# Block-sparse attention with a maxout layer: a written-out task order, and 86 tasks on other engines

## The chip, the core and the metric

The kernel runs on one core of a Trainium2 chip. The core has TensorE (PE in the profile; its weight loads are listed apart as PEld), VectorE (DVE), ScalarE (ACT), GpSimd (POOL) and SyncE (SP), which here only issues DMAs. Each engine works through its own list of instructions in order; between engines there are only semaphore waits. The metric is the device time in microseconds of one execution. "Span" is the time from the first to the last instruction in the profile of one execution; the execution's own time is a little longer.

## The reference

Attention over 4 batches, 8 heads, 768 positions and head dimension 64. Each query sees the keys within 15 positions of it, and, for all 24 blocks of 32 positions, one key that is the maximum over the block and one value that is the mean over the block, with log(32) added to the block's score. Behind it stands a maxout layer on 3072 tokens.

```python
k_sum = k.reshape(B, H, nb, block, D).max(axis=3)          # block = 32, nb = 24
v_sum = v.reshape(B, H, nb, block, D).mean(axis=3)
scores_l = scale * q @ k.T, kept where |pos_q - pos_k| < 16
scores_s = scale * q @ k_sum.T + log(block)
a = softmax(concat([scores_l, scores_s]))
x = (a @ concat([v, v_sum])) with heads side by side         # 3072 x 512
h1, h2 = x @ w1, x @ w2                                      # 512 x 1024 each
out = maximum(h1, h2) @ w_out                                # 1024 x 512
```

## The kernel before

The program is written as 776 tasks. A task has an engine, an estimated duration, a function that issues its instructions, a label, and the buffers that it reads and writes (`Plan.op`, line 123). Buffers come out of rings of slots (`Ring`, line 42): six for loaded k and q (`kqf`), four for loaded v (`vf`) and for weights (`wf`), four for turned k (`kx`) and q (`qx`), eight PSUM banks (`banks`), and so on. `Plan.run` (line 155) walks over time in steps of 0.02 us, starts on every idle engine the task of the best priority whose inputs and slots are free by its estimates, gives its buffers their slots, and so gets an order. It then calls the tasks' functions in that order (line 187). An engine's instruction list is the order in which the functions were called; waits between engines follow from the data and from the slots.

Labels carry batch and head pair (b, hp: "k12" is k of batch 1, head pair 2), and for later work batch and a third of the positions (grp, 256 positions each). The stages are:

- **Loads** on SP, in one queue: `load k`, `load q` (lines 362, 367), `load v` (373) for each batch and head pair, 384 KB each; `load w0`, `load w1` (693), twice each, 1 MB (columns 0 to 511 of w1 and of w2, then columns 512 to 1023 of both); `load wo0`, `load wo1` (726). A load needs a free slot, that is, the cast of what stood there before must be done.
- **Preparing k and q** (`prep`, 515): `cast` to bf16, `turn` (transposes on TensorE, 543, or for some pairs of batches 2 and 3 by DMA, 505 and 510), `place` (PSUM to `kx` or `qx`), `max k` (block maxima, VectorE, 562), `wrap`, `tails` and `sums k` (copies inside `kx`).
- **Preparing v** (`cast_v`, 384; `spread_v`, 392): `cast v`, for batches 1 to 3 `ones` (a memset on GpSimd, 402), `odd v` (three shifted copies), `sums` (block means on TensorE, 427 and 432, and a copy out) and `all sums` (the means laid beside every window). The sums of batches 1 to 3 need all four casts of v of their batch.
- **Attention**: `scores` (TensorE, 600, for batch 0 with the mask added by 591), `exp` (ScalarE, 625), `mask` (VectorE, 632, batches 1 to 3), `values` (TensorE, 648), `inv` and `x` (VectorE, 659 and 661: the division by the sum), `turn x` (TensorE, 674, or DMA, 666) and `xt` (copy of the turned x out of PSUM).
- **Weights**: `wd n` = w2 - w1 for a quarter n of the columns (700), `w1b n` (cast), `turn w1 n` (714; for n = 2 on f32, straight from the loaded `wf`), `w1t n` (copy out of PSUM), `wo n` (cast of w_out), and `w1o` = w1 @ w_out (741, two TensorE tasks and one copy for each quarter). The layer is computed as relu(x @ wd) @ w_out + x @ w1o.
- **The layer** (`maxout`, 749): `hidden b grp n` (757), `relu` (ScalarE, 762), `out` (`out_part`, 772: one TensorE task on w1o, line 778, and two on w_out, line 785), `copy out` and the store (806, 808). The last tile of all is cut into column groups of 256, 128 and 128.
- **Fillers**: 40 `idle` matmuls on zeros (829), put where TensorE has nothing else to do; all lie in the first 25 us.

Copies are made by one helper (`copy`, line 485), so that in the profile most casts, places and moves on all three engines carry line 490 and are told apart by their tiles.

`CFG` holds one letter for each group of copies, which chooses its engine, and priorities and corrections to them (`bump`), from which the planner makes the order.

Of the kernel before, what the change touches and what calls it, by code (L numbers as in the profile page):

```python
# [16 lines left out]
ACT = mybir.ActivationFunctionType  # L17
# [2 lines left out]

CFG = dict(
    smc="CCC",
    kd="....D..DD.DD", xd="D...DD.DD.DDDDDDDD", tus=(1.6, 1.0, 1.2), kc="ADDA", qc="APPP", kp="DADD", qp="DDDA",
    tl="AADA", od="DADP", se="DADA", sr="DPdP", vc="ADPA", sc=4, s0=4, ph=1, ph0=2, av=4, lkp="DDDA", lxt="DADAAD",
    idle=40, pz=1, wd="PPDD", w1b="DPFD", w1t="AAAA", wo="PAAD", xt="DDDDDA", kv=(0.2, 1.2, 4.2, 4.2), sp=0.7,
# [11 lines left out]
    },  # L37
)
ENG = {"D": "DVE", "A": "ACT", "P": "POOL"}


class Ring:
# [70 lines left out]
class Plan:  # L113
# [9 lines left out]
    def op(self, engine, us, fn, read=(), write=(), change=(), touch=(), behind=(), prio=0.0, label="", port=False):  # L123
        t = Task()
        t.engine, t.us, t.fn, t.label = engine, us, fn, label
        t.port = engine == "POOL" or port and engine == "DVE"
        t.prio = (prio + CFG["bump"].get(label, 0), len(self.tasks))
        t.new, t.behind = [*write, *change], behind
        t.deps = {w for b in (*read, *change) for w in b.writers}
        for b in t.new:  # L130
            b.writers.append(t)
        for b in (*read, *touch, *t.new):
            b.users.append(t)
        self.tasks.append(t)
        return t
# [19 lines left out]
    def run(self):  # L155
        waiting = {e: [] for e in self.LAG}
        for t in sorted(self.tasks, key=lambda t: t.prio):
            waiting[t.engine].append(t)
        busy = dict(self.BEGIN)
        self.held = {"POOL": 0.0, "DVE": 0.0}  # L160
        sent = [0.0] * self.DEPTH
        gate = Gate(1.0)
        order, tick = [], 0
        while len(order) < len(self.tasks):
            now = tick * 0.02
            for e, queue in waiting.items():
                if busy[e] > now or (e == "SP" and sent[-self.DEPTH] > now):
                    continue
                t = next((t for t in queue if self.ready(t, now)), None)
                if t is None:  # L170
                    continue
                t.start = now
                if e == "SP":
                    busy[e] = now + self.ISSUE
                    end = max(sent[-1], now + self.FIRST) + t.us
                    sent.append(end)
                    t.done = end + max(0.0, min(1.5, 0.6 * (end - 2.3), 0.4 * (14.0 - end)))
                else:
                    end = gate.end(now, t.us) if e == "PE" else now + t.us
                    busy[e] = t.done = end  # L180
                    if t.port:
                        self.held[e] = t.done
                queue.remove(t)
                order.append(t)
            tick += 1
            assert now < 1000, [t.label for q in waiting.values() for t in q]
        for t in order:
            t.fn()
        return order

# [2 lines left out]
def kernel(  # L193
# [14 lines left out]
    nc = tc.nc  # L208
    B, H, S, D = 4, 8, 768, 64
# [10 lines left out]
    op = plan.op  # L220
# [132 lines left out]
    kqin, kx, qx, xt = {}, {}, {}, {}  # L353
# [131 lines left out]
    def copy(engine, us, aps, label, port=True, halves=False, **kw):  # L485
        engine = ENG[engine]
        us = us if isinstance(us, float) else us[engine[0]]
        def fn():
            for o, i in [aps(0), aps(1)] if halves else [aps()]:
                {"DVE": nc.vector.tensor_copy, "ACT": nc.scalar.copy,  # L490
                 "POOL": nc.gpsimd.tensor_copy}[engine](out=o, in_=i)
        op(engine, us, fn, label=label, port=port, **kw)

    def on(e):
        return {"DVE": nc.vector, "POOL": nc.gpsimd}[e]
# [192 lines left out]
    def load_w12(half, prios, prio, prio_t):  # L688
        fs = []
        for w, at in zip((moe_w1, moe_w2), prios):  # L690
            f = Buf(wfr)
            fs.append(f)
            op("SP", 2.9, lambda f=f, w=w: nc.sync.dma_start(  # L693
                out=f.ap[:],
                in_=w.rearrange("(c p) n -> p c n", p=128)[:, :, 512 * half:512 * half + 512]),
               write=[f], prio=at, label=f"load w{half}")
        for n in (2 * half, 2 * half + 1):
            part = lambda f, at=256 * (n % 2): f.ap[:, :, at:at + 256]
            e = CFG["wd"][n]
            op(ENG[e], {"D": 1.23, "P": 2.3}[e], lambda n=n, part=part, e=e: on(ENG[e]).tensor_tensor(  # L700
                out=wd[n].ap[:], in0=part(fs[1]), in1=part(fs[0]), op=ALU.subtract),
               read=fs, write=[wd[n]], prio=prio + n % 2, port=True, label=f"wd {n}")
            whole = CFG["w1b"][n] == "F"
            if not whole:
                copy(CFG["w1b"][n], {"P": 1.05, "A": 1.06, "D": 0.75}, lambda n=n, part=part: (w1b[n].ap[:], part(fs[0])),
                     read=fs[:1], write=[w1b[n]], prio=prio + n % 2, label=f"w1b {n}")
            ps = Buf(banks, "x", 2 if whole else 1)

            def turn(n=n, ps=ps, whole=whole, part=part):
                src, to, one = (part(fs[0]), bank(ps, 1024), ident32) if whole else (  # L710
                    w1b[n].ap, bank(ps, 1024, BF16), identity)
                for f in range(2):
                    for c in range(KC):
                        nc.tensor.transpose(  # L714
                            out=to[:, (f * KC + c) * 128:(f * KC + c) * 128 + 128],
                            in_=src[:, c, 128 * f:128 * f + 128], identity=one[:])
# [184 lines left out]
```

## Time and profile before

| what | value |
|---|---|
| median of 3 runs | 170.58 us (170.07, 170.58, 171.06) |
| the profiled execution's own time | 170.39 us |
| span of the profiled execution | 168.7 us |
| granted TensorE clock | 1.00 |
| instructions in the profile | 4452 |
| HBM read, written | 25.17 MB, 6.29 MB |
| VectorE, ScalarE, GpSimd busy | 104.0, 93.0, 42.9 us |

The page of the profile gives busy times and shares of the span, the chain of work that ended last (each step followed back to what released it), groups of instructions by line with their mean duration, and DMA issues. In the chain, "SPq" is the time that SP's queue needs to issue a DMA, "DMA" the time until the data is there, "issue" the engine's own time between instructions. Matmul ends are modelled: two matmuls one behind the other overlap in the listing, so spacing from start to start says more than the listed length. The trace also has the moments at which each transfer landed; the first loads landed at 3.95 us (k00) to 18.90 (v03), the four weight loads at 22.61, 25.32, 28.29 and 30.93, then q10 31.99, k10 33.17, v10 34.55, k11 35.56, q11 36.54, wo0 39.22, wo1 42.04, v11 43.75, k12 44.76, q12 46.61, v12 48.33, q13 49.41, k13 50.53, v13 52.31, k20 54.06, q20 55.86, v20 56.96, k21 58.72, q21 59.80, v21 62.13, q22 63.18, k22 64.16, v22 66.61.

Medians of some durations on each engine, from the trace (us):

| task | VectorE | ScalarE | GpSimd |
|---|---|---|---|
| cast k | 0.59 | 1.05 | 0.94 |
| cast q, cast v | 0.55 | 0.83 | 0.83 |
| place k | 0.55 | 0.80 | |
| place q | 0.95 | 0.80 | |
| xt | 0.42 | 0.59 | |
| wrap, tails | 0.16, 0.25 | 0.21, 0.51 | 0.38, 0.51 |
| odd v 0, 1, 2 (batch 0) | 0.36, 0.66, 0.44 | 0.83, 0.72, 0.29 | 1.03, 0.71, 0.29 |
| all sums (batches 1 and 2) | 1.26 | | |
| wd, w1b | 1.22, 0.67 | | 2.36, 1.04 |
| wo | 0.69 | 1.05 | 1.04 |
| w1o (copy) | 0.69 | | |

### The profile page before, as it was taken

The page shows a single profiled execution, that of the slowest core. Times are in us where ns is not written, and L with a number is a line of the kernel's source. Part 1 is how long each engine was busy: PE and PEld are TensorE (multiplying, and loading weights), DVE is VectorE, ACT ScalarE, POOL GpSimd, SP SyncE. Part 2 cuts the span into 40 slices and gives each one's busy share as a digit, 9 for nine tenths or more (in the row PEclk, how much of TensorE's full clock was granted, in tenths as well). Part 3 has the DMA queues.
Part 4 walks back from the last instruction along what each step waited for, and adds up shares of the span by engine and source line. Part 5 has one row for each costly group of instructions (what it writes and reads, how often), then busy time and mean ns, then how long its engine had stood idle before and what let it go on. Part 6 is the DMA issues. An engine that isn't in the chain of part 4 may idle for free.

```text
span 168.7 us, 4452 instructions
## 1 busy us (share of the span) xinstructions
PE 158.6 (94%) x1819; PEld 104.4 (62%) x1819; DVE 104.0 (62%) x224; ACT 93.0 (55%) x146; POOL 42.9 (25%) x73
## 2 busy tenths in 40 slices
PE   4797896999999999999999999999999999999992
PEld 2665565998464655577484675865747658746661
DVE  6799997999569996758994744839438360000001
ACT  3767872789851766346185584681764716424420
POOL 7824889142215150036202010116020000000000
PEclk9999999999999999999999999999999999999999
DMA  5999999999999999999699999965753527011113
GB/s 170 314 316 283 336 389 376 304 348 342 301 294 216 264 334 292 189 239 162 128 271 334 260 203 194 241 155 116 200 102 99 125 59 163 0 62 73 55 62 124
DMA packets 69397, 35.82 MB, mean 212 GB/s; under 512 B 56577, under 2 KB 63361, under 8 KB 69377
## 3 DMA queue, kind: packets, MB, share of 16 engines
q1 hardware_dynamic: 65856, 29.38, 75.5%
q10 hardware_dynamic: 3520, 6.16, 11.6%
q8 instruction: 14, 0.23, 0.6%
q14 instruction: 7, 0.05, 0.1%
HBM read 25.17 MB, written 6.29 MB: 186 GB/s over the span
## 4 chain that ended last, share of the span: by engine, by line
PE 73%; SPq 9%; DVE 7%; DMA 7%; issue 2%; DVEq 0%
PE banks L757 24%; PE banks L785 22%; PE banks L778 10%; DMA wf<-in_moe_w_dram 7%; SPq L367 4%; PE banks L741 4%; PE banks L648 3%; PE banks L600 3%; SPq L373 3%; DVE vx L490 3%; PE banks L543 2%; SPq L693 2%; PE banks L714 1%; PE banks L674 1%; DVE qx L490 1%
## 5 line engine op out<-in xcount | busy, mean ns | idle before, releaser
L785 PE MATMUL banks<-wo,g 128*128 128x512 bf16 (+2 forms) x208 | 46.9, 363 | 0.0
L757 PE MATMUL banks<-xt,wd 128*128 128x256 bf16 x384 | 46.4, 273 | 0.0
L757 PEld LDWEIGHTS <-wd 128*128 128x128 bf16 x384 | 36.7, 98 | 6.5 <-issue 0.2
L762 ACT ACTIVATE g<-banks 128x512 bf16<-128x512 f32 x48 | 28.0, 602 | 14.2 <-PE banks L757 14.0
L794 ACT COPY o<-banks 128x512 f32<-128x512 f32 x23 | 13.5, 586 | 32.0 <-PE banks L785 31.0
L785 PEld LDWEIGHTS <-g 128*128 128x128 bf16 x208 | 18.4, 98 | 17.7 <-issue 0.2
L778 PE MATMUL banks<-w1o,xt 128*128 128x512 bf16 (+2 forms) x104 | 23.7, 363 | 0.0
L490 POOL CAST kqb<-kqf 128x768 bf16<-128x768 f32 x12 | 11.3, 942 | 37.5 <-PE banks L543 18.5
L625 ACT ACTIVATE pba<-banks 128x1024 bf16<-128x1024 f32 x16 | 16.4, 1025 | 6.0 <-PE banks L600 5.6
L632 DVE TENSOR_TENSOR pba<-pba,mask 128x1024 bf16<-128x1024 bf16 x12 | 8.5, 706 | 15.4 <-ACT pba L625 15.3
L490 DVE COPY o<-banks 128x128 f32<-128x128 f32 x2 | 0.6, 292 | 26.8 <-PE banks L785 26.8
L661 DVE TENSOR_TENSOR xs<-banks,inv 128x512 bf16<-128x512 f32 x24 | 16.3, 687 | 0.6
L778 PEld LDWEIGHTS <-xt 128*128 128x128 bf16 x104 | 9.8, 98 | 8.8
L562 DVE TENSOR_REDUCE ks<-kx 128x24 bf16<-128x768 bf16 x16 | 15.0, 945 | 0.1
L490 POOL CAST vx<-vf 128x768 bf16<-128x768 f32 x7 | 5.9, 843 | 22.5 <-DMA vf<-in_v_dram 22.4
L600 PEld LDWEIGHTS <-kx 64*128 64x128 bf16 x416 | 7.3, 96 | 6.7 <-issue 5.7
L490 ACT CAST kqb<-kqf 128x768 bf16<-128x768 f32 x9 | 7.9, 881 | 5.7 <-DMA kqf<-in_k_dram 2.0
L490 POOL COPY kx<-kx 128x32 bf16<-128x32 bf16 (+1 forms) x12 | 6.2, 520 | 16.3 <-DMA kx<-kqb 10.3
L829 PE MATMUL banks<-zeros 128*128 128x256 bf16 x40 | 8.4, 336 | 1.8 <-DVE zeros L826 1.8
L625 ACT ACTIVATE pbb<-banks 128x512 bf16<-128x512 f32 x16 | 9.6, 603 | 0.8 <-ACT o L794 0.8
L490 DVE COPY vx<-vx 64x3168 bf16<-64x3168 bf16 (+5 forms) x15 | 9.9, 676 | 0.2
L600 PE MATMUL banks<-qx,kx 64*128 64x64 bf16 (+2 forms) x416 | 9.4, 190 | 0.0
(85 smaller groups left out, 184.1 us busy)
## 6 DMA issues: line engine op xcount, KB each, us to landing
kqf<-in_k_dram SPq DMA_DIRECT2D x16, 384.0 KB, 6.7
kqf<-in_q_dram SPq DMA_DIRECT2D x16, 384.0 KB, 5.8
vf<-in_v_dram SPq DMA_DIRECT2D x16, 384.0 KB, 6.8
out_dram<-o ACTq DMA_DIRECT2D x19, 256.0 KB, 3.9
wf<-in_moe_w_dram SPq DMA_DIRECT2D x4, 1024.0 KB, 10.2
wf<-in_moe_w_out_dram SPq DMA_DIRECT2D x2, 1024.0 KB, 7.5
out_dram<-o ACTq DMA_DIRECT2D x4, 224.0 KB, 3.3
vx<-sums SPq DMA_DIRECT2D x4, 99.0 KB, 3.7
```

The costliest lines, as they stand in the source:

```text
L490: {"DVE": nc.vector.tensor_copy, "ACT": nc.scalar.copy, "POOL": nc.gpsimd.tensor_copy}[engine](out=o, in_=i)
L562: op("DVE", 0.95, lambda: nc.vector.tensor_reduce(out=ks.ap[:], in_=free(kt(), 128, [256, NM], [192, 2], [32, 2], [1, 32]), axis=AX.X, op= ...
L600: nc.tensor.matmul(out=bank(ps[i], 1024)[:, 512 * a + at + n0:512 * a + at + n1], lhsT=kx[b, hp].ap[r, 128 * t + 128:128 * t + 256], rhs=q ...
L625: op("ACT", (1.03, 0.6)[i], lambda: nc.scalar.activation(out=pv(), in_=bank(ps, 1024).rearrange("p (a c) -> p a c", a=2)[:, :, 0:64 * n], ...
L632: op("DVE", (0.69, 0.43)[i], lambda: nc.vector.tensor_tensor(out=pv(), in0=pv(), in1=m, op=ALU.mult), read=[mask_in], change=[pb], prio=pr ...
L661: op("DVE", 0.69, lambda: nc.vector.tensor_tensor(out=x.ap[:], in0=av()[:, :, :, 0:D], in1=inv.ap[:].to_broadcast([128, 2, 4, D]), op=ALU. ...
L757: nc.tensor.matmul(out=bank(ps)[:, 256 * s:256 * s + 256], lhsT=wd[n].ap[:, c, 128 * s:128 * s + 128], rhs=x.ap[:, c, :], start=(c == 0), ...
L762: op("ACT", 0.6, lambda n=n, ps=ps: nc.scalar.activation(out=g.ap[:, 2 * n:2 * n + 2, :].rearrange("p f n -> p (f n)"), in_=bank(ps), func ...
L778: nc.tensor.matmul(out=bank(ps, c1 - c0), lhsT=x.ap[:, c, sl], rhs=w1o[c].ap[:, cols], start=(c == 0), stop=False)
L785: nc.tensor.matmul(out=bank(ps, c1 - c0), lhsT=g.ap[:, f, sl], rhs=wo[f // 2].ap[:, f % 2, cols], start=False, stop=(f == FC - 1))
L794: nc.scalar.copy(out=aps()[0], in_=aps()[1])
L829: nc.tensor.matmul(out=bank(ps, 256), lhsT=zeros[:, 0:128], rhs=zeros[:], start=True, stop=True)
```

## The change

The planner still runs and still gives every buffer its slot. Then its order is thrown away: a tuple `ORDER` of the 776 task numbers says in which order the functions are called. A dictionary `done_by` names 86 tasks whose copy (for wd 1 and wd 3 the subtraction) is made by another engine than the letters in `CFG` say: 26 go from VectorE to ScalarE, 16 from VectorE to GpSimd, 13 from ScalarE to VectorE, 12 from GpSimd to VectorE, 12 from GpSimd to ScalarE, 7 from ScalarE to GpSimd. No instruction is added or removed.

```diff
 CFG = dict(
     smc="CCC",
+    done_by={
+        "cast v00": "DVE", "odd v000": "POOL", "odd v001": "ACT", "odd v002": "POOL", "odd v020": "DVE",
+        "odd v021": "DVE", "odd v022": "POOL", "odd v040": "ACT", "odd v041": "POOL", "odd v042": "ACT",
+        "cast v03": "DVE", "odd v060": "DVE", "wd 1": "DVE", "wd 3": "POOL", "w1b 3": "POOL", "w1t 3": "DVE",
+        "wo 2": "POOL", "cast k00": "DVE", "place k00": "ACT", "wrap k00": "POOL", "tails k00": "DVE",
+        "place q00": "ACT", "cast k01": "ACT", "cast q01": "ACT", "place k01": "DVE", "place q01": "ACT",
+        "cast k02": "POOL", "cast q02": "ACT", "place k02": "ACT", "wrap k02": "POOL", "place q02": "ACT",
+        "cast k03": "POOL", "cast q03": "DVE", "place k03": "ACT", "tails k03": "POOL", "xt 000": "ACT",
+        "xt 020": "ACT", "xt 001": "ACT", "xt 021": "ACT", "xt 002": "ACT", "cast v10": "DVE", "cast v11": "POOL",
+        "place k10": "ACT", "cast k11": "POOL", "place q11": "DVE", "xt 102": "ACT", "wrap k12": "ACT",
+        "tails k12": "DVE", "place q12": "ACT", "cast k13": "ACT", "place k13": "DVE", "wrap k13": "DVE",
+        "tails k13": "DVE", "place q13": "ACT", "cast v20": "ACT", "cast v22": "POOL", "cast v23": "DVE",
...
+        "cast q33": "ACT", "wrap k33": "ACT", "w1o 1": "ACT", "w1o 2": "ACT",
+    },
...
+ORDER = (
+    60, 12, 61, 6, 62, 14, 8, 15, 16, 2, 71, 4, 0, 3, 19, 72, 9, 13, 21, 23, 73, 128, 82, 129, 130, 17, 26, 25, 132,
...
+    763, 764, 765,
+)
...
             tick += 1
             assert now < 1000, [t.label for q in waiting.values() for t in q]
+        order = [self.tasks[i] for i in ORDER]
+        assert len(set(ORDER)) == len(self.tasks)
         for t in order:
+            t.engine = CFG["done_by"].get(t.label, t.engine) if t.engine in ENG.values() else t.engine
             t.fn()
         return order
...
             for o, i in [aps(0), aps(1)] if halves else [aps()]:
                 {"DVE": nc.vector.tensor_copy, "ACT": nc.scalar.copy,
-                 "POOL": nc.gpsimd.tensor_copy}[engine](out=o, in_=i)
+                 "POOL": nc.gpsimd.tensor_copy}[CFG["done_by"].get(label, engine)](out=o, in_=i)
...
-            op(ENG[e], {"D": 1.23, "P": 2.3}[e], lambda n=n, part=part, e=e: on(ENG[e]).tensor_tensor(
+            op(ENG[e], {"D": 1.23, "P": 2.3}[e], lambda n=n, part=part, e=e: on(CFG["done_by"].get(f"wd {n}", ENG[e])).tensor_tensor(
                 out=wd[n].ap[:], in0=part(fs[1]), in1=part(fs[0]), op=ALU.subtract),
```

Read as labels, the numbers give these orders in the stretches that matter below.

```text
SP, loads behind the first 16 (which keep their order: k00 q00 v00 k01 q01 v01 k02 q02 k03 q03 v02 v03 w0 w0 w1 w1)
before: q10 k10 v10 k11 q11 wo0 wo1 v11 k12 q12 v12 q13 k13 v13 k20 q20 v20 k21 q21 v21 q22 k22 v22 k23 ...
after:  k11 k10 q10 wo0 wo1 k12 q11 v11 k13 v13 v12 v10 q12 k20 q13 v21 q20 q21 q22 v20 k22 v22 (turn k200, k201) v23 ...
SP later, after: ... (turn q23) k31 (turn x201) q32 k32 q31 v30 (turn k301, k300, q30, x221, q32, k320) k33 ...

TensorE around the first hidden tasks
before: values 020, turn x001, values 021, turn w1 1, turn x020, values 002, turn w1 2, turn x021, values 022,
        hidden 000, turn x002, hidden 001, turn w1 0, hidden 011, 002, 003, turn w1 3, hidden 010, turn x022, turn k10, ...
after:  values 020, turn x001, values 021, turn w1 1, values 002, turn x020, values 022, turn x021, turn x002, turn w1 2,
        hidden 000, turn w1 0, hidden 001, 011, 010, 002, turn w1 3, hidden 012, turn k10, turn x022, hidden 003, 013,
        turn q10, hidden 021, turn k11, hidden 020, scores 10, w1o 0, 2, 1, 2, turn q11, w1o 1, 0, 3, 3, scores 11,
        hidden 022, out 010, turn k12, out 010, sums 10, out 001, turn q12, out 001, out 011, out 001, turn q13, scores 12,
        out 011, turn k13, out 010, out 011, values 101, hidden 023, values 100, out 020, turn x101, out 020, values 102, ...

VectorE from w1o to the x of batch 1
before: w1o 0, 1, 2, cast v12, w1o 3, place k12, mask 110, 111, max k12, place q12, cast v13, sums k12, odd v100, 101, 102,
        place q13, all sums 100, 101, mask 120, 121, max k13, inv 100, inv 101, x 100, x 101, ...
after:  place q11, cast v13, w1o 0, w1o 3, cast v12, cast v10, mask 101, odd v102, place k12, odd v100, max k12, sums k12,
        tails k12, mask 111, odd v101, mask 100, all sums 101, 100, mask 110, place k13, cast q20, wrap k13, inv 101,
        tails k13, x 101, max k13, inv 100, sums k13, x 100, ...

ScalarE from the first places to w1t 2, after: cast q00, place k00, place q00, cast k01, odd v001, cast q01, exp 000, place q01,
        exp 001, wrap k01, cast q02, tails k01, sums 02, place k02, place q02, place k03, place q03, exp 010, wrap k03, exp 011,
        odd v042, odd v040, exp 021, sums 06, exp 030, exp 020, exp 031, xt 000, xt 001, w1t 1, xt 020, xt 021, w1t 2, ...
```

In the last tile of all, the TensorE tasks of the two 128-column groups now come first, and the 256-column group, which ScalarE copies and stores, comes last.

More of the change, by code (lines that the diff above doesn't have):

```diff
@@ L22 @@
     smc="CCC",
+    done_by={
[10 more added lines that the diff above has]
+        "tails k13": "DVE", "place q13": "ACT", "cast v20": "ACT", "cast v22": "POOL", "cast v23": "DVE",
+        "cast k20": "ACT", "tails k20": "ACT", "cast k21": "POOL", "tails k21": "POOL", "cast k22": "DVE",
+        "wrap k22": "ACT", "tails k22": "ACT", "place q22": "ACT", "cast k23": "ACT", "wrap k23": "DVE",
+        "cast v31": "ACT", "cast v32": "DVE", "cast k30": "POOL", "cast q30": "POOL", "wrap k30": "ACT",
+        "tails k30": "POOL", "cast k31": "POOL", "cast q31": "DVE", "wrap k31": "POOL", "tails k31": "POOL",
+        "place q31": "DVE", "cast k32": "ACT", "cast q32": "DVE", "wrap k32": "DVE", "tails k32": "ACT",
+        "cast q33": "ACT", "wrap k33": "ACT", "w1o 1": "ACT", "w1o 2": "ACT",
+    },
     kd="....D..DD.DD", xd="D...DD.DD.DDDDDDDD", tus=(1.6, 1.0, 1.2), kc="ADDA", qc="APPP", kp="DADD", qp="DDDA",
```

33 rows, old and new, of the table ORDER are left out of this document.

## The prediction

> **What bounds the kernel now.** I read the busy shares first, then the chain of waits in order of time, then the busy time by stage, then the TensorE timeline where a stage is not full.
>
> ```profile
> PE 158.6 (94%) x1819; PEld 104.4 (62%) x1819; DVE 104.0 (62%) x224; ACT 93.0 (55%) x146; POOL 42.9 (25%) x73
> ```
>
> TensorE is the fullest engine, but 94% is no proof: 40 of its matmuls are fillers on zeros, and ends are modelled. The chain says more.
>
> ```profile
> 16.87 11.43 DMA wf<-in_moe_w_dram
> 28.29 0.04 issue
> 28.34 1.09 PE banks L714 x8
> 29.43 0.22 PE banks L674 x4
> 29.65 0.37 PE banks L648 x16
> 30.03 0.98 PE banks L757 x8
> 31.00 0.22 PE banks L674 x4
> 31.23 0.87 PE banks L757 x8
> ```
>
> Up to 28.3 us the chain is loads: the first 16 transfers land one behind the other from 3.95 to 30.93 us, and the third weight load, which the f32 transposes of task "turn w1 2" (L714) need, lands at 28.29. TensorE issues in order, so it stands there for 1.08 us with other work queued behind. From 28.34 on the chain is almost only TensorE. The windows (columns: length, busy PE, PEld, DVE, ACT, POOL, clock, DMA share, GB/s) show how full it is:
>
> ```profile
> 28.30:49.60 21.30, 21.26 (x236) 16.04 (x237) 16.28 (x30) 16.20 (x24) 5.69 (x6) 1.00 1.10 325
> 49.60:63.80 14.20, 13.83 (x145) 8.01 (x144) 13.98 (x25) 6.71 (x11) 5.98 (x9) 1.00 1.12 271
> 63.80:84.00 20.20, 20.20 (x218) 12.43 (x219) 14.62 (x29) 9.14 (x15) 5.18 (x8) 1.00 1.12 196
> 84.00:120.00 36.00, 36.00 (x448) 23.68 (x446) 24.44 (x53) 21.69 (x36) 5.88 (x8) 1.00 1.12 221
> 120.00:165.50 45.50, 45.50 (x460) 29.28 (x457) 9.37 (x21) 20.95 (x35) 0.87 (x2) 1.00 0.35 90
> ```
>
> One gap is left, in the second window, where VectorE is full (13.98 of 14.20). The TensorE timeline has it:
>
> ```profile
> 62.38 1.03 PE L778 MATMUL banks<-w1o,xt 128*128 128x512 bf16 x4
> 63.78 0.40 PE L674 MATMUL banks<-identity,xs 128*128 128x128 bf16 x4 [0.37 <-DVE xs L661]
> ```
>
> Four such matmuls elsewhere occupy 0.863 us from start to start; here 1.399 pass, so the wait for task "x 101" is 0.53 us (the 0.37 counts from modelled ends). So the end is 28.34 plus TensorE's own work plus 0.53. What I call a cost below is this start-to-start spacing, taken from the trace between 28 and 162 us, where it repeats to 0.01: hidden 0.873, out or w1o 0.863, scores 0.461, values 0.376, turn x 0.223, turn k 0.327, turn q 0.335, sums of batches 1 to 3 0.778; 0.095 more for a task of whole-array matmuls ahead of one of half-array ones (scores, values, sums), 0.011 more behind one, 0.12 less for a values task directly behind another. With these the old order makes 136.32 us after 28.34; with the gap, and 0.3 for the last matmul, that ends at 165.5, as measured.
>
> **The change part by part.** Nothing is added to or removed from TensorE; only its order changes.
>
> (a) Before "turn w1 2" the list now also has turn x021, values 022 and turn x002: 0.223 + 0.376 + 0.223 = 0.82 us that falls into the wait for the load. Behind it, the entries into half-array work drop from 27 to 25 (2 x 0.106 = 0.21 less) and the values pairs from 6 to 5 (0.12 more). New sum 135.41: a gain of 0.91.
>
> This holds only if all that stands before it is ready by 28.3. The 16 first transfers keep their order. VectorE's work up to "x 002" falls from 25.95 to 21.01 us (medians of the same copies by engine), as the xt copies and places go to ScalarE. I walked the new lists with rows. ScalarE becomes the full engine: from cast k01 at 8.3 us through exp 000, the places of head pairs 2 and 3, and six exps, it ends exp 031 at about 24.8 (before: 24.76); xt 000 and xt 001 (0.59 each) end at 26.0, w1t 1 at 27.0, xt 020 at 27.6. VectorE's x 002 ends at about 27.8 (before 28.44), so turn x002 is out at about 28.2. Cover left: 0.1 to 0.2 us. POOL has wd 0 at 27.8 as before, wd 1 moves to VectorE and ends at 29.0 (before 30.07), and "hidden 001" wants it at 30.6. Without this cover, the first thing late is "turn w1 2" itself, one for one.
>
> (b) The 0.53 us wait for "x 101". Around it VectorE gives w1o 1, w1o 2, place q12 and place q13 (0.69, 0.69, 0.95, 0.95) to ScalarE, and takes cast v10, place k13 and place q11 (0.55, 0.55, 0.95), and the wraps and tails of k13 and tails of k12 (0.16, 0.25, 0.25). From cast v10 through x 100 its medians sum to 13.98; the same way of summing gives 14.57 for the old stretch w1o 3 through x 101, which took 14.11, so I take 13.5. Cast v10 begins when v10 lands, and v10 is now the twelfth load behind the first 16, not the third. Continuing the landings at the spacings of before (k or q 1.05 to 1.1, v 1.75, the two wo loads 2.7 and 2.8) from 30.93: wo1 39.7, v11 43.4, v13 46.2, v12 48.0, v10 49.75. Then x 100 ends at 63.3; values 102, which takes over its banks, is due at 63.77. So the gap goes: gain 0.53, and the new cover is 0.4.
>
> (c) New waits. Everywhere the new order is closer to its producers than the old. By the same walk: hidden 021 wants xt 022, which ends at 38.0 on ScalarE behind place k10, at 38.03 (0 to 0.2 lost); sums 10 wants cast v10 and POOL's ones 1 behind it (50.5 to 51.4) at 51.5; scores 22 wants x 201 (95.0) at 95.3; sums 30 wants v30, whose load stands behind "turn x201" in SP's queue (SP issues q32, k32, q31, v30 after 95.1; landing about 106, cast 0.83 and ones 3 after it, 108.2) at 108.7; hidden 303 wants turn x320 (a transpose of 3.6 us from issue to landing, as before) at about the moment that it lands (0 to 0.2). The bounds for the sum of these are 0, if every step keeps its time, and about 3 us, if the loads slip as in the second rival; the rows put most of them just on the good side, so I take 0.5.
>
> VectorE's and POOL's copies hold each other up. Beside POOL's two copies the 0.16 us wrap of k02 took four times as long and ended with them:
>
> ```profile
> 16.51 1.75 POOL L490 COPY vx<-sums 32x792 bf16<-32x792 bf16 x2
> 17.66 0.62 DVE L490 COPY kx<-kx 128x32 bf16<-128x32 bf16 x1
> ```
>
> The Trainium skill (SBUF — State Buffer, Who interferes with whom) says why: both engines share one port pair, a VectorE copy in a two-port mode and a GpSimd instruction exclude each other, and the second to start waits out the whole of the first. The trace agrees (18.28 against 18.26). A plan made of single durations does not see it.
>
> (d) The end. The last group is now the 256-column one: ScalarE's copy (0.37) and store of 128 KB (1.7 to landing) in place of VectorE's 0.29 and 64 KB (1.7). About 0.1 either way; I take 0.
>
> Sum: -0.91 - 0.53 + 0.5 = -0.94. The profiled execution took 170.39 (span 168.7), so it would take 169.45. It lay 0.19 under the median of the three runs, 170.58; against that, 169.6.
>
> **Rivals.**
> 1. The start takes the gain back (about 170.4). ScalarE is full from 8 to 28 us and the cover is 0.1 to 0.2. POOL has 22 tasks and 20.4 us before wd 0 ends, against 18 and 19.1; four more meetings at the shared time, each worth 0.2 to 0.5 on VectorE, make x 002 about 0.8 us late and undo most of (a). For it: VectorE copies of one shape vary in the trace (0.34 to 0.98, 0.16 to 0.65). Against it: VectorE has 5 us less to do there. By the rule of the Trainium skill (SBUF — State Buffer, Who interferes with whom) alone, every meeting costs the loser the rest of the other's copy, up to 1.03 here, which would give the same 170.4 or a little more.
> 2. Slower: v10 comes too late. VectorE waits in order at cast v10, and behind it stand mask 101, place k12, the odd copies, both all sums, masks 100 and 110 and every x of batch 1; TensorE waits for sums 10 and values 102. It decides once v10 lands after about 50.1. Four v loads stand in that stretch; some of before took 2.3 to 2.4 us in place of 1.75 (v21, v22), which makes 4 x 0.6 = 2.4 late, 2.0 after the cover, and the same at v30 would add up to 0.8. Then 169.6 + 2.0 to 2.8 gives 171.6 to 172.4; I put it at 171.9. Against it: most v loads of before kept 1.1 to 1.8, and the transfers are the same in bytes.
> 3. The list does nothing that counts (170.5): slots still come from the planner and engines run by their waits, so the gap of (b) only moves. Against it: (a) is work that visibly stood behind a wait.
>
> **How the numbers follow.** Forecast 0.52, rival 1 0.20, rival 2 0.22, rival 3 0.06. The forecast's own range is 168.95 + 0.15 = 169.1 (no new wait at all) to 170.1. More gain has no source, since TensorE's sum after the load is fixed. Range for 8 in 10: 168.9 to 172.0, from the forecast's low end less the scatter of runs to the middle of rival 2. What a measurement can tell from no change is about 0.5%, 0.85 us. Below 169.73 lie most of the forecast and none of the rivals: faster 0.46. Within 0.5%, the rest of the forecast, rivals 1 and 3: 0.31. Slower: rival 2: 0.23.
>
> **What would show it.** Right: L714's f32 group still begins at about 28.3, with values and turn x tasks directly before it and hidden (L757) directly behind; no idle TensorE time before xs at 62 to 64; the last matmul at about 164.5. Wrong in (a): that group begins later than 28.6, released by xs on VectorE. Wrong in (c): idle TensorE time put down to vx or xs near 51, 64 or 108, with a v load landing just before.

## The result, and the profile after

The changed kernel is 0.9% faster where it is compared: its counted executions take 0.9911 of the time of the kernel before, with a 95% interval of 0.9881 to 0.994 (22 executions of each taken side by side). The counted executions of the change lie between 168.91 and 169.91 us, median 169.31; the forecast was 169.6, its own range 169.1 to 170.1. The comparison leaves 13 of the 22 executions of the change (171.5 to 174.9 us) out as disturbed; over all 22 the change has a median of 172.66, more than the 171.07 of the kernel before. The profiled execution, 171.5 us with a span of 169.8, is one of the 13, so its start need not be that of a counted execution. By the ratio, the counted executions of the kernel before stand here at about 170.8 (169.31 / 0.9911), 0.2 us more than the 170.58 that the prediction started from.

The busy shares of the changed kernel:

```profile
PE 155.7 (92%) x1801; PEld 103.9 (61%) x1819; DVE 99.8 (59%) x207; ACT 100.2 (59%) x164; POOL 43.7 (26%) x72
```

VectorE gave 4.2 us away and ScalarE took 7.2 more. TensorE's busy time fell by 2.9 although it does the same work: 18 matmul records are missing, so this number says nothing. The windows of the changed kernel, with the columns of before (length, busy PE, PEld, DVE, ACT, POOL, clock, DMA share, GB/s):

```profile
28.30:49.60 21.30, 19.98 (x207) 15.35 (x209) 16.17 (x26) 14.34 (x23) 9.85 (x9) 1.00 1.05 294
49.60:63.80 14.20, 13.99 (x153) 8.30 (x153) 11.67 (x25) 9.72 (x15) 0.82 (x1) 1.00 1.17 284
```

The second stretch is what step (b) was about: VectorE is busy for 11.67 of 14.20 us in place of 13.98. Most of that fall comes from the window: this execution is about 1.5 us late there (turn x101 at 65.18 in place of 63.78), so the same 14.20 us hold other work, and in a kernel below that is not late there (the one with turn x002 back, turn x101 at 63.60) VectorE is busy for 13.23. The first stretch holds a surprise: more than a microsecond of TensorE time is gone right at its beginning. The timeline of the changed kernel from 22 to 32 us shows why (columns: start, length, engine, line, operation; in brackets the idle time before it and what ended that):

```profile
24.93 0.69 DVE L721 TENSOR_TENSOR xs<-banks,inv 128x512 bf16<-128x512 f32 x1
25.25 2.35 POOL L760 TENSOR_TENSOR wd<-wf,wf 128x1024 bf16<-128x1024 f32 x1
25.54 2.62 DVE L550 CAST w1b<-wf 128x1024 bf16<-128x1024 f32 x1
...
29.05 0.40 PE L734 MATMUL banks<-identity,xs 128*128 128x128 bf16 x4 [1.52 <-DVE xs L721]
...
30.97 1.04 PE L774 MATMUL banks<-ident,wf 128*128 128x128 f32 x8
```

VectorE's cast w1b 0, which took 0.65 in the profile before, took 2.62 here: it met GpSimd's wd 0 and ended at 28.16, 0.55 after it (27.61). Behind it on VectorE stand the x tasks that the new order wants before turn w1 2 (L774), so this group began at 30.97 and not at 28.3, though its load had landed at 27.80. The part of the chain of waits of the changed kernel that leads there (start, length, what; "issue" is time without a visible cause):

```profile
25.62 0.35 DVE w1b L550
25.97 2.11 issue
28.08 0.21 DVE inv L719
...
30.74 0.40 PE banks L734 x4
31.13 0.88 PE banks L774 x8
```

The 2.11 us of "issue" lie inside the cast's own 2.62 us (25.54 to 28.16): the chain names no releaser for them, and that wd 0 is the cause is so far read only from the overlap. By the prediction's own sign for it (a group that begins later than 28.6, released by xs on VectorE), step (a) went wrong in this execution. Behind it the list runs as forecast. In the TensorE timeline of the changed kernel the place of the old gap, turn x101, has none, and the last matmul group ends at 166.49:

```profile
64.31 1.04 PE L838 MATMUL banks<-w1o,xt 128*128 128x512 bf16 x3
65.18 0.39 PE L734 MATMUL banks<-identity,xs 128*128 128x128 bf16 x4
...
165.45 1.04 PE L845 MATMUL banks<-wo,g 128*128 128x256 bf16 x8
```

From 30.97 to 166.49 are 135.52 us; TensorE's own work by the prediction was 135.41 + 0.3. So from the f32 group on nothing is lost in this execution. The counted executions have spans of 167.2 to 168.2; less the 3.3 us from the last matmul to the end, and less 135.5, turn w1 2 began between 28.4 and 29.4 in them. That is worked out and not seen, since no counted execution was profiled.

### The profile page after: what moved, and what is told of

Its sections match the earlier page's. It is cut to its first block, busy times and chain, and to the rows that moved or that the text cites. A ratio compares the mean times of both kernels' runs of the same rounds, so it can differ in the third digit from the quotient of the medians.

```text
span 169.8 us, 4403 instructions
## 1 busy us (share of the span) xinstructions
PE 155.7 (92%) x1801; PEld 103.9 (61%) x1819; DVE 99.8 (59%) x207; ACT 100.2 (59%) x164; POOL 43.7 (26%) x72
## 4 chain that ended last, share of the span: by engine, by line
PE 80%; DVE 5%; DMA 5%; issue 3%; SPq 2%; ACT 2%
PE banks L817 25%; PE banks L845 23%; PE banks L838 12%; PE banks L801 4%; PE banks L660 4%; PE banks L708 4%; DMA vf<-in_v_dram 4%; PE banks L603 3%; SPq L427 2%; DVE vx L550 2%; PE banks L487 1%; DVE xs L721 1%; ACT pba L685 1%; DMA out_dram<-o 1%; PE banks L774 1%
## 5 line engine op out<-in xcount | busy, mean ns | idle before, releaser
L845 PE MATMUL banks<-wo,g 128*128 128x512 bf16 (+2 forms) x201 | 45.2, 362 | 0.9 <-issue 0.8
L822 ACT ACTIVATE g<-banks 128x512 bf16<-128x512 f32 x48 | 27.2, 600 | 20.2 <-PE banks L817 18.4
L845 PEld LDWEIGHTS <-g 128*128 128x128 bf16 x208 | 19.0, 98 | 17.7
L838 PE MATMUL banks<-w1o,xt 128*128 128x512 bf16 (+2 forms) x94 | 23.0, 361 | 0.8 <-issue 0.5
L550 POOL CAST kqb<-kqf 128x768 bf16<-128x768 f32 x11 | 10.8, 991 | 49.0 <-DMA kqf<-in_k_dram 29.4
L838 PEld LDWEIGHTS <-xt 128*128 128x128 bf16 x104 | 9.3, 98 | 8.6 <-issue 0.2
L550 ACT CAST kqb<-kqf 128x768 bf16<-128x768 f32 x13 | 11.2, 871 | 5.5 <-DMA kqf<-in_q_dram 3.3
L550 ACT COPY xt<-banks 128x512 bf16<-128x512 bf16 x10 | 5.9, 589 | 8.6 <-PE banks L734 8.6
L719 DVE RECIPROCAL inv<-banks 128x8 f32<-128x8 f32 x24 | 4.7, 201 | 9.7 <-PE banks L708 8.1
L692 DVE TENSOR_TENSOR pbb<-pbb,mask 128x512 bf16<-128x512 bf16 x12 | 5.0, 416 | 7.4 <-ACT pbb L685 7.4
```

The lines of the kernel that those rows point to most:

```text
L550: {"DVE": nc.vector.tensor_copy, "ACT": nc.scalar.copy, "POOL": nc.gpsimd.tensor_copy}[CFG["done_by"].get(label, engine)](out=o, in_=i)
L692: op("DVE", (0.69, 0.43)[i], lambda: nc.vector.tensor_tensor(out=pv(), in0=pv(), in1=m, op=ALU.mult), read=[mask_in], change=[pb], prio=pr ...
L822: op("ACT", 0.6, lambda n=n, ps=ps: nc.scalar.activation(out=g.ap[:, 2 * n:2 * n + 2, :].rearrange("p f n -> p (f n)"), in_=bank(ps), func ...
L838: nc.tensor.matmul(out=bank(ps, c1 - c0), lhsT=x.ap[:, c, sl], rhs=w1o[c].ap[:, cols], start=(c == 0), stop=False)
L845: nc.tensor.matmul(out=bank(ps, c1 - c0), lhsT=g.ap[:, f, sl], rhs=wo[f // 2].ap[:, f % 2, cols], start=False, stop=(f == FC - 1))
```

## The experiments

All ratios are to the kernel before, from executions on the same chip.

### The change once more, and the blocked cast moved

The first run is the changed kernel again, without an edit.

> The changed kernel once more, for a second profile. In the first profile w1b 0 (VectorE, f32 cast of 128x1024) took 2.62 us, from 25.54 to 28.16, while POOL ran wd 0 from 25.25 to 27.61, and turn w1 2 began at 30.97. Theory P (shared port, whichever starts first): it is a race of about 0.3 us; where w1b 0 starts before wd 0 it takes 0.7 to 0.9, turn w1 2 begins at 28.0 to 28.8 and the span is 167.0 to 167.8. Rival D (VectorE simply has too much in front of x 002): turn w1 2 begins near 31 again and the span is 169.8 again. Ratio to before 0.991 by both, since it is a repetition.

Measured: 0.9906 (0.9861 to 0.9952), counted executions 169.38 to 169.54. The profile came out with the blocked cast again: w1b 0 from 25.79 to 28.41, wd 0 from 25.51 to 27.86, turn w1 2 at 31.55. It adds no picture of a start without the meeting, but it shows what can follow from one. TensorE stood for 1.52 us ahead of turn x020 in both profiles of the change; in this one the granted clock then fell, with 0.79 as the mean of 28 to 36 us and 1.00 before and behind (columns as above):

```profile
28.00:36.00 8.00, 6.25 (x64) 5.79 (x65) 7.86 (x12) 4.13 (x7) 5.15 (x3) 0.79 0.86 294
```

The f32 group took 1.91 us in place of 1.04, and the span is 171.6 in place of 169.8. What decides whether the clock falls is open, since it did not in the first profile.

The second run moves the cast on VectorE (fences that name tasks like this one show their order by labels, not lines of code):

```diff
-x 001, w1b 0, inv 020, x 020, inv 021, x 021, inv 002, x 002, wd 1
+x 001, inv 020, x 020, inv 021, x 021, inv 002, x 002, w1b 0, wd 1
```

> Only w1b 0 moved in VectorE's order, from behind x 001 to behind x 002, where wd 0 is over. Theory P: w1b 0 takes about 0.7, x 002 ends at 27.3 to 28.0, turn w1 2 begins at 27.8 to 28.4 (when the third weight load has landed), span 166.8 to 167.5, ratio to before 0.984 to 0.990, with no run near the slow end of the unchanged one. Rival D: x 002 comes 0.7 earlier than in the unchanged one and no more, turn w1 2 begins near 30, ratio 0.99 to 1.0.

Measured: 0.9935 (0.9902 to 0.9969), so no gain over the change in counted executions, and outside the theory's 0.984 to 0.990. But the cast takes 0.68 again, and the profile comes nearer to the start that the prediction described: x 002 ends at 28.57 and turn w1 2 begins at 28.86. The timeline of this kernel also shows the next meetings:

```profile
28.49 0.68 DVE L554 CAST w1b<-wf 128x1024 bf16<-128x1024 f32 x1
28.55 1.52 POOL L554 CAST w1b<-wf 128x1024 bf16<-128x1024 f32 x1 [0.83 <-DMA wf<-in_moe_w_dram]
...
29.09 2.06 DVE L764 TENSOR_TENSOR wd<-wf,wf 128x1024 bf16<-128x1024 f32 x1
```

Now the cast w1b 0 begins 0.06 us ahead of a GpSimd cast and keeps its length, and the GpSimd cast takes 1.52 in place of 1.04. The subtraction wd 1 begins behind that GpSimd cast and takes 2.06 in place of the 1.22 that it takes alone. This is cheaper, because only hidden 001 waits for wd 1, for less than 0.2 us. What cost this execution more was a wait of 0.75 us at 113.8, which the TensorE timeline puts down to g from ScalarE; ScalarE stood at wrap k30, whose transposes by DMA landed at 111.30 where they had landed at 109.59 in the profile of the change.

### That wait taken away, and turn x002 moved back

The next kernel keeps the moved cast and puts wrap k30 two ScalarE tasks later:

```diff
-wrap k30, copy out 121, cast k32
+copy out 121, cast k32, wrap k30
```

> The changed kernel with w1b 0 behind x 002 (as in the run with w1b 0 later) and, besides, ScalarE's wrap k30 moved behind cast k32, so that a late transpose of k30 does not hold up the copies of g at 111 to 114 us. Theory (the 0.75 us wait of TensorE at 113.8 us in the run with w1b 0 later is ScalarE standing at wrap k30): no idle TensorE time between 105 and 118 us, and the ratio is 0.988 to 0.991 where that run had 0.9935. Rival (that late transpose was one execution's accident, or wrap k30 is wanted soon after): 0.992 to 0.995, as in that run.

Measured: 0.9922 (0.9887 to 0.9958), 169.69 us over all its executions; no idle TensorE time between 105 and 118 us in its profile, although the transpose landed late again (111.02). The wait is explained, but the ratio is in the rival's range: such a late transpose does not come in every execution (107.97 in the profile of the next kernel). On top of it, turn x002 goes behind hidden 000, where it stood before the change:

```diff
-turn x002, turn w1 2, hidden 000
+turn w1 2, hidden 000, turn x002
```

> As the run with wrap k30 later, and turn x002 moved back behind hidden 000, so that the f32 transposes of turn w1 2 no longer need x 002 from VectorE. Theory (x 002 at 28.5 sets when turn w1 2 begins): turn w1 2 begins at 28.3 in place of 28.8; 0.22 us of work goes back behind it; net gain 0.1 to 0.3 us: ratio 0.001 to 0.002 below the run with wrap k30 later. Rival (values 022 and turn x021 set the begin just as much): turn w1 2 begins at 28.6 or later and the time is 0.1 to 0.3 us longer than in that run.

Measured: 0.9913 (0.9883 to 0.9944), 169.83 us. Against the run before it the difference is within the intervals. TensorE's timeline ahead of the f32 group:

```profile
28.52 0.44 PE L712 MATMUL banks<-vx,pbb 128*64 128x65 bf16 x16
28.94 0.38 PE L738 MATMUL banks<-identity,xs 128*128 128x128 bf16 x4
29.16 1.04 PE L778 MATMUL banks<-ident,wf 128*128 128x128 f32 x8
```

The load had landed at 27.82. No wait is left in front of the group, not for x 002 and not for the load: TensorE itself comes there late. So the rival's condition (28.6 or later) came true, and no worth of the third task in front of the load shows.

### The first step undone, in the changed kernel and done alone before it

The same kernel, with the other two tasks moved back as well. ScalarE's copy xt 021 keeps its place in the list and so stands ahead of turn x021 in this kernel: it copies what the bank held before, at the same size. So this kernel leaves out one turned tile, and the hidden tasks on that copy have one wait less; it is of use for the time of TensorE's start alone.

```diff
-values 022, turn x021, turn w1 2, hidden 000
+turn w1 2, turn x021, values 022, hidden 000
```

> As the run with turn x002 back, and turn x021 and values 022 moved back behind turn w1 2 too, as in the kernel before: the first step of the prediction undone in the changed kernel, 0.6 us more behind the load. Theory (the step's gain was read from one execution in which TensorE stood for 1.08 us; in this list TensorE comes to turn w1 2 only when the load has landed or later, so there was hardly a wait to fill): turn w1 2 begins at 28.4 to 28.7 in place of 29.16, most of the 0.6 us is got back, and the ratio is 0.991 to 0.994, within 0.0025 of that run. Rival (the step is worth its 0.6 to 0.9 us here too, since the load lands at 28.6 or later): turn w1 2 begins with 0.4 us or more of idle TensorE time ahead of it and the ratio is 0.995 to 0.997.

Measured: 0.9948 (0.9922 to 0.9973), 170.15 us. Its TensorE timeline has the wait that the kernel before had:

```profile
27.06 0.40 PE L738 MATMUL banks<-identity,xs 128*128 128x128 bf16 x4
28.34 1.09 PE L778 MATMUL banks<-ident,wf 128*128 128x128 f32 x8 [0.88 <-DMA wf<-in_moe_w_dram]
```

The difference to 0.9913 is 0.0035, 0.6 us, the 0.22 + 0.38 of the two tasks; that is what the rival said, although its 0.995 was missed by a hair. Each ratio is uncertain by 0.003, so the difference is not clear of the noise. By the two medians it is 0.3 us (170.15 against 169.83, on different chips), by the last matmul's end in the two profiles 0.45 (165.36 against 164.91). The same two tasks moved ahead of turn w1 2 in the kernel before, with nothing else:

> The kernel before with one change to its order: turn x021 and values 022 stand ahead of turn w1 2, so they run while TensorE waits for the third weight load. Nothing else moves, no engine changes. Theory (the step of the prediction that moves work into the wait is right by itself): 0.22 + 0.38 us leave the work behind the load, so turn w1 2 still begins at 28.3 to 28.4 and the last copy out is 0.55 to 0.7 us earlier than 166.4 (DVE at 165.9): ratio 0.9955 to 0.997. Rival (the wait isn't free, because values 022 then waits for its inputs and pushes turn w1 2 back one for one): turn w1 2 begins at 28.8 or later and the ratio is 0.999 to 1.002.

Measured: 0.9987 (0.9948 to 1.0027). This decides for neither. In the profile turn w1 2 begins at 29.10, as the rival has it, but the whole start was later in this execution (turn x000 at 25.07; 24.05 in the profile before), and behind the load the order did gain: at the first relu the execution was only 0.11 us behind the profile before, 0.66 us caught up. It then lost 0.79 us at 111 us, for the reason that the next run shows.

### The second step alone

The kernel before with its own order, and a done_by of four entries:

```diff
+    done_by={"w1o 1": "ACT", "w1o 2": "ACT", "place q12": "ACT", "place q13": "ACT"},
```

> The kernel before with its own order, and only w1o 1, w1o 2, place q12 and place q13 moved from VectorE to ScalarE. Theory (the 0.53 us wait of turn x101 is VectorE being full): x 101 ends 2 us or more earlier than at 63.72, the wait is gone, and the end is 0.4 to 0.55 us earlier: ratio 0.9968 to 0.9978. Rival (a planner's order that was made for the old engines does not fit the new ones; ScalarE holds up something else): the gap at 62 to 64 us goes but another of the same size shows within 20 us, with vx, g or qx from ScalarE named as what it waits for: ratio 0.999 to 1.004.

Measured: 0.9983 (0.9947 to 1.0019), between the two ranges. X 101 ends at 62.53, 1.2 us earlier and not 2. The gap at turn x101 is gone (the four out matmuls at 62.77, turn x101 at 63.63, the spacing of 0.86 that such a group has everywhere), and a gap of the same size is elsewhere, as the rival said, but 47 us later. In the timeline of this kernel, ScalarE's queue and TensorE:

```profile
108.36 1.54 ACTq L848 DMA_DIRECT2D out_dram<-o  x1
109.94 0.80 ACT L530 COPY qx<-banks 128x768 bf16<-128x768 bf16 x1 [1.99 <-PE banks L797]
...
110.79 0.53 PE L640 MATMUL banks<-qx,kx 64*128 64x64 bf16 x26 [0.51 <-ACT qx L530]
```

In the profile before, the same store issue took 0.44:

```profile
108.52 0.44 ACTq L808 DMA_DIRECT2D out_dram<-o  x1
109.00 0.80 ACT L490 COPY qx<-banks 128x768 bf16<-128x768 bf16 x1 [0.89 <-PE banks L757]
```

ScalarE issues the stores of its own copies. Place q31 stands behind such an issue, and scores 31 waits for place q31. In the run with two tasks early the issue took 1.79 and the wait 0.79. The new done_by has place q31 on VectorE; so the next run adds this fifth copy to the four:

```diff
+    done_by={"w1o 1": "ACT", "w1o 2": "ACT", "place q12": "ACT", "place q13": "ACT", "place q31": "DVE"},
```

> As the run with four copies (the kernel before, w1o 1, w1o 2, place q12, place q13 on ScalarE), and place q31 moved from ScalarE to VectorE. Theory (in the runs with four copies and with two tasks early the 0.51 and 0.79 us of idle TensorE time at 111 us came from place q31, which stood on ScalarE behind the issue of a store that took 1.54 and 1.79 us in place of 0.44): no idle TensorE time before scores 31 nor before turn x101, ratio 0.994 to 0.997, and all runs near each other. Rival (another wait takes its place, or the gap is rare): ratio 0.998 to 1.001, as in the run with four copies.

Measured: 0.9969 (0.993 to 1.0008), with a median of 170.63 against 171.16 in counted executions. No idle time before scores 31 or turn x101; a wait of 0.53 us for a transpose by DMA stands at 139.6 us in this execution. The store's issue took 0.45 us in it, so this profile could not have shown the wait at scores 31 in any case. The point value is in the theory's range, but the interval reaches 1 and the executions spread over 2 us, so that place q31 behind a long store issue costs time is likely and not shown.

### Order and engines apart

One run has the new ORDER with the old engines (done_by empty), one the new engines with the planner's order.

> The written-out order with the engines of before. If the gain comes from the order of TensorE alone (three tasks ahead of the load's wait), the ratio is 0.990 to 0.995. If the moved copies are what makes these tasks ready in time: VectorE's work up to x 002 is 26 us by medians in place of 21, x 002 ends near 30 to 31, turn w1 2 begins near 31, and the wait for x 101 is back, so 171 to 174 us, ratio 1.00 to 1.02.

> The 86 tasks on their new engines, in the planner's order of before. If the engines alone make the gain, the ratio is 0.990 to 0.995. If it needs the order too: turn w1 2 still stands ahead of turn x021, values 022 and turn x002, so the 0.8 us of these is not saved; the 0.53 us wait at x 101 may go; copies that POOL or ScalarE now do in places planned for another engine are late by up to 1 to 2 us in the first 28 us. Ratio 0.997 to 1.015.

Measured: the order alone 1.0157 (1.0122 to 1.0191), the engines alone 1.0061 (1.0024 to 1.0098). With the order alone VectorE still has the xt copies, so x 002 ends at 30.02 and turn w1 2 begins at 30.31, and later TensorE waits twice for VectorE, for its copy of qx and for a mask. From its timeline:

```profile
62.90 0.32 PE L690 MATMUL banks<-vx,pba 128*64 128x65 bf16 x8 [0.91 <-DVE qx L532]
63.86 0.32 PE L690 MATMUL banks<-vx,pba 128*64 128x65 bf16 x8 [0.65 <-DVE pba L674]
```

This profile also has the case that both profiles of the change lacked, w1b 0 beginning ahead of wd 0:

```profile
26.09 0.76 DVE L532 CAST w1b<-wf 128x1024 bf16<-128x1024 f32 x1
26.27 2.78 POOL L742 TENSOR_TENSOR wd<-wf,wf 128x1024 bf16<-128x1024 f32 x1
```

Here VectorE's cast takes 0.76, and GpSimd's wd 0 takes 2.78 in place of 2.35: of the same two instructions the other one loses. So who begins first decides, as the expectation of the first run had it: the cast began 0.18 us ahead of wd 0 here, and 0.29 and 0.28 behind it in the two profiles of the change.

With the engines alone turn w1 2 begins at 28.57, but scores 10 comes at 42.34 in place of 41.13 in the profile before, and about as much is still there at the last hidden task (144.80 and 143.62). The timeline names a wait of 0.35 for a wd from GpSimd at 34.9, which took 3.39 us: VectorE's subtraction had begun 0.04 us ahead of it (31.39 against 31.43) and kept its 1.23. The rest of the second was not resolved. Each half alone makes the kernel slower; only together they gain.

### Later v10, and a lighter VectorE at the start

To price the second rival, the kernel with turn x002 back got its load v10 two loads later:

```diff
-load v10, load q12, load k20
+load q12, load k20, load v10
```

> As the run with turn x002 back, and the load v10 moved behind load q12 and load k20 in SP's order, so that it lands about 2.8 us later (near 52.5 in place of 49.9). Theory (the second rival of the prediction has the right mechanism, and only did not come about): VectorE stands at cast v10 in order, sums 10, x 101, x 100 and values 102 are late one for one behind a cover of about 0.4 us, so the time is 1.5 to 2.4 us over that run: ratio 1.000 to 1.005 to the kernel before. Rival (VectorE has room there now that it is no longer full, and takes the delay up): less than 0.7 us over that run, ratio 0.991 to 0.995.

Measured: 0.9986 (0.9952 to 1.002), 170.88 us. V10 landed at 52.94 in place of 49.99. TensorE's timeline has one wait for it, ahead of sums 10, and none at turn x101 or values 102:

```profile
53.67 0.84 PE L491 MATMUL banks<-vx,amean 128*64 128x256 bf16 x12 [1.33 <-DVE vx L554]
```

Of 2.95 us, 1.33 came through, and the ratio rose by 0.0073, 1.25 us. Both theories hold half of it: cast v10 does hold up what stands behind it, but 1.6 us are absorbed. In the kernel with turn x002 back the cast ended at 50.74 and TensorE came to sums 10 at 52.51; so, with the 0.15 us from the cast's end to sums 10 in the late run (53.52 to 53.67), that is where the 1.6 us lie.

The last kernel tried to speed up the start: all sums 041, one of the two copies of 0.97 us ahead of x 000, goes to ScalarE.

```diff
+        "all sums 041": "ACT",
```

> As the run with turn x002 back, and the copy all sums 041 moved from VectorE to ScalarE. Theory (what holds up the start is VectorE's row of copies from 20 to 28 us, two of which, 0.97 us each, stand ahead of x 000): x 000 begins near 23.8 in place of 24.78, TensorE comes to turn w1 2 0.5 to 0.9 us earlier, at 28.3 to 28.6 where the third weight load lands, and the time is 0.4 to 0.8 us under that run: ratio 0.987 to 0.989. Rival (ScalarE, which is as full there, passes the delay on through exp 030 and exp 020): turn w1 2 at 29.0 or later, ratio 0.991 to 0.993.

Measured: 0.9925 (0.9896 to 0.9955), 169.64 us: no gain. X 000 begins at 24.49, because all sums 040 then waits for ScalarE's copy, which ends at 23.46; turn w1 2 begins at 28.87, between the two expectations, and the ratio is the rival's. Its timeline shows the cast w1b 0 meeting GpSimd once more:

```profile
28.82 1.04 POOL L554 CAST w1b<-wf 128x1024 bf16<-128x1024 f32 x1 [0.89 <-PE banks L712]
...
28.94 1.47 DVE L554 CAST w1b<-wf 128x1024 bf16<-128x1024 f32 x1
```

It ended at 30.41, with nothing urgent behind it.

No kernel here beats the change in counted executions. Those with w1b 0 behind x 002 and nothing made worse (the cast moved, wrap k30 later, turn x002 back, all sums 041 moved) come near it there, with 0.9913 to 0.9935, and over all executions taken their medians are 169.6 to 170.2 us against 172.66. Of the 29 executions of the changed kernel in its two runs 17 took 171.5 us or more; of the 69 in the six runs with the cast moved 2 did. So the meeting likely makes most of the long executions of the change, though only two of them were profiled. The kernel with turn x002 back is the one to keep.

## Why the prediction was right, and where its terms were not

**The time.** 169.6 was forecast and 169.31 measured. The gain was forecast as 0.57% and is 0.89% (0.6% to 1.19%). The profiled execution of the kernel before, 170.39 us, was better than its median of 171.07 over all executions here, so a sum made against that execution leaves out what an average one loses besides. That the sum came so near is in part luck: (a) was put too high and the loss of (c) as well, with opposite signs. Even with (b) at its full 0.53, the terms as they came out below make a gain of 0.8 to 1.1 us; the measured one is 1.5 (from 170.8 to 169.31), and the rest has no term in the prediction. And all this holds for the counted executions alone: the two profiled executions, which are not among them, went the way of the first rival and beyond its 170.4 (171.5 and 173.35).

**(a), forecast -0.91: likely right in kind, too large.** Filling the wait for the load gains up to the 0.6 us of two tasks (0.9948 with them moved back, 0.9913 with them in front; 0.3 by the medians and 0.45 in the profiles; by the ratios alone it is not clear of the noise). The third task adds nothing that shows, since TensorE comes to turn w1 2 with no time left. The step that failed is the length of the wait: 1.08 us was read from one execution, and it was the longest of the three with the start of the kernel before. Turn x000 began at 24.05 there; in the two runs with the old order and, up to 40 us, the old engines (four and five copies), at 24.90 and 25.59, and the wait ahead of the f32 group, which began at 28.72 in both, was 0.62 us in the first and none in the second. A wait for a fixed landing is worth only what the chain ahead leaves of it, and that chain scatters by over 1 us.

**The cover of (a), "x 002 at about 27.8, 0.1 to 0.2 us".** With the cast moved, x 002 ended at 28.57, later than forecast, but TensorE was late too. In the profiled one the cast w1b 0, which my walk took at its old length, met wd 0 on GpSimd and cost 2 us. That is the first rival's mechanism, at a place and a price it did not have: it put the most that one meeting can cost at 1.03 us and four of them at about 0.8, and wd 0 takes 2.35. The prediction's citation stands: the Trainium skill (SBUF — State Buffer, Who interferes with whom) says that who issues first has the shared ports for the whole instruction and the other is fully blocked. The trace agrees: w1b 0 ended 0.55 us after wd 0 (28.16 against 27.61) and, in the run with all sums 041 on ScalarE, 0.55 us after GpSimd's cast (30.41 against 29.86), which is nearly its own length of 0.67. It was the same 0.55 in the second profile of the change (28.41 against 27.86) and with two tasks early (31.18 against 30.63).

**(b), forecast -0.53: the wait went, its worth alone is not shown.** Turn x101 has no wait in the change, nor with four copies. The landing of v10, forecast for 49.75, was 49.91 to 50.51 in the five profiles with the cast moved and this load in its place. But the four copies alone measured 0.9983: in that profile the half microsecond came back at scores 31. That wait is likely latent in the kernel before, whose profiled execution had a quick store issue. The new list removes it as well, by place q31, which the prediction passed over. This is a likely source of what the change gained beyond the forecast, together with (c); it was seen in profiles only.

**(c), forecast +0.5 between 0 and 3: about 0.** TensorE's 135.52 us behind the load leave no room for waits in the profile of the change. They exist, as the 0.75 us at 113.8 in the run with the cast moved shows, but not in each execution.

**(d), forecast 0: right.** From the last matmul's end to the end of the span there are 3.3 us, and 3.2 before (165.50 to 168.7).

**The rivals.** The second, v10 too late, did not happen: nothing waits for it, not even where it landed later than the 50.1 at which this rival was to decide (50.43 and 50.51 in two profiles). Its mechanism is real, but the cover is about 1.6 us and not 0.1 at sums 10 and 0.4 behind. TensorE comes to sums 10 at 52.51 in the kernel on which the late load was tried, 1 us later than the walk had it, and its start was 0.8 us late (turn w1 2 at 29.16 in place of 28.34). The third, a list that does nothing, falls with order and engines alone at 1.0157 and 1.0061.

## What to carry to other kernels

A slack read from one profile is one draw: before filling a wait, look at how far the chain ahead of it scatters, for instance by profiling a kernel whose edit lies later. A list of tasks planned with single durations should keep VectorE's casts from SBUF away from GpSimd's long copies, or put in front of the urgent ones nothing that can be blocked; a shift of half a microsecond changes who loses, so one good profile does not clear such a list. When a copy is taken off a full engine, follow the next engine in order too, with the DMA issues that stand in its queue.

## What the hardware did that was not expected

The issue of one small store (32 KB) by ScalarE took 0.44, 1.54 and 1.79 us in three kernels with the same order at that place, while SP was issuing a transpose by DMA (from 108.11 to 109.95 in the second; the store's issue ended at 109.90). In the first SP issued such a transpose as well (108.26 to 110.43; the store's issue ended at 108.96), so what decides is open.

A VectorE subtraction of two tiles in SBUF was slowed by GpSimd too (2.06 against 1.22). The Trainium skill (SBUF — State Buffer, Who interferes with whom) says that an instruction of VectorE with two inputs from SBUF contends with a GpSimd instruction that reads SBUF; the trace agrees. In the run with the cast moved the subtraction ended 1.07 us after GpSimd's cast (31.14 against 30.07), and 1.07 to 1.08 after it in three other kernels. Only one side lost in each of these meetings, the one that began second: with the engines alone VectorE's subtraction began first, and GpSimd's took 3.39 in place of 2.36. VectorE's x tasks, which read PSUM, kept 0.69 us beside wd 0 in the same profiles.
